# Two steps of the routing three slots later, in blocks 2 to 6

## The chip, the cores and the metric

One core of one Trainium2 chip runs the kernel. The metric is device microseconds of one execution. Engines are named as in the profile: PE (TensorE's products), PEld (its weight loads), DVE (VectorE), ACT (ScalarE), POOL (GpSimd) and SP (SyncE, which issues most DMAs).

## What is computed

Three layers in a row, over 3072 tokens of width 384:

```python
# 1: a recurrent attention, per batch (4) and head (8), 768 steps, head size 48
cur = u * k_t (outer) v_t
y_t = r_t @ (state + cur)
state = w_t[:, None] * state + k_t (outer) v_t
# 2: a gated layer, d_ff 1536
xn = x / sqrt(mean(x * x) + 1e-6) * rms_g
x = (silu(xn @ w_gate) * (xn @ w_val)) @ w_out
# 3: eight experts, each token goes to one
logits = x @ w_gate;  e_idx = argmax(logits)
gate_w = softmax(logits)[e_idx];  eom = sigmoid(x @ w_output_gate)
out[mask_e] = gate_w * eom_e * (relu(x @ w1[e]) @ w2[e])
```

## The kernel before

The tokens are cut into 24 tiles of 128, and these into eight blocks of three tiles (`for j in range(NB)`). Block j runs the gated layer on its own three tiles and, in between, the attention of the three tiles of block j + 1. The gated layer walks over 12 chunks f of d_ff: `l1` multiplies x with w_gate and then with w_val (two halves of nine products each, all at L181), and from f = 2 on `l2` multiplies the result of chunk f - 2 with w_out (nine products, also L181) into three accumulators of width 400. Each product that needs full precision is done as three with a high and a low part.

The order on every engine is written by hand. `l1` and `l2` call `slot()` at fixed points: after each half of a chunk and, from f = 2 on, after `l2`. Slots are counted from 0 in each block: 0 and 1 belong to f = 0, 2 and 3 to f = 1, 4, 5 and 6 to f = 2 (6 is behind the first `l2`), 7, 8 and 9 to f = 3, and so on. A `Plan` holds a list of generators for each slot and advances each by one step there. Whatever a step issues stands in the engines' queues at that point.

Two kinds of generators are planned in blocks 1 to 6. `attention` has nine steps per tile; its offsets are `OFFS` = 0, 1.6, 3.2, 4.8, 6.4, 8, 9.6, 11.6, 13.8, cut to whole slots, and the second and third tile start at slots 9 and 18. In short, for a tile from block 1 on: step 0 a scan on DVE (L382) and two products r, k and u on POOL (L390, L391); step 1 L394 and L395 on DVE; step 2 the second scan (L403, L406), a sum (L413), and on POOL the bonus y (L425); step 3 four transposes (L435) and L453; step 4 the scores (L461, PE) and their masks (L465, DVE); step 5, which is slot 8 for the first tile, the products that make y: with the state (L489), of the masked scores with v (L496) and of the keys with v (L478), then L504 on DVE, L508 and L510 on ACT and L513 on POOL; step 6 L520; step 7 L528 on ACT; step 8 three transposes (L532), L536 on ACT and L539 on DVE.

`route` sorts the tokens of the block before into the experts' areas. Its first step is one product with `acc` (L632, PE) and nine small operations on DVE (L639 to L657), which find each token's expert. Its second step is four products (L660, L663) that count the tokens ahead of each, seven small operations on DVE (L668 to L677), and three scatters, each a memset (L256) and an indirect DMA (L257) on POOL, which put the rows of 394 numbers, 128 at a time, into the scratch tensor `scr`. The two steps stand four slots apart. The call in block j gives the first step's slot: 24 in block 1 and 2 in all later ones. Block 7 has no attention left.

PSUM tiles of the name m come from three banks in turn, so each user waits for the reader of the third one before it.

After the eight blocks the experts run, one after another, on rows fetched from `scr`; the change does not touch them.

Of the kernel before, what the change touches and what calls it, by code (L numbers as in the profile page):

```python
# [22 lines left out]
def kernel(  # L23
# [14 lines left out]
    WINDOWS=((448,), (424,), (408,), (396,), (384,), (368,), (352,)),  # L38
    ROUTE_AT=(0, 3),
    ROUTE_STEP=3,  # L40
    WHOLE=6,
    KV_AT=0,
    KT_DVE=(0, 2, 3, 4, 5),
# [61 lines left out]
    def bank(tag, bufs, shape):  # L105
        return ps.tile(shape, F32, tag=tag, bufs=bufs, name=tag)

    def words(src):
        return src.bitcast(U32) if src.dtype != U32 else src
# [440 lines left out]
    def route_columns(k, tf):  # L550
# [11 lines left out]
        for i in range(2):  # L562
            for kk in range(KD):
                for t in (slice(0, 64), slice(64, P)):
# [3 lines left out]
                    )  # L568
        if k < WHOLE:
            nc.scalar.activation(out=whole_w[k][:, :, DM:WIDTH], in_=o, func=AF.Copy)  # L570
# [55 lines left out]
    def route(c, t0, nt, xr, last):  # L626

        b_ps = bank("m", 3, [P, E])
        nc.tensor.matmul(b_ps, c["one_b"], c["acc"], start=True, stop=True)  # L632
        base = late.tile([P, E], F32, tag="base", name="base")
        if last:
            nc.vector.tensor_tensor(out=base, in0=b_ps, in1=c["floor"], op=ALU.max)
            nc.vector.tensor_tensor(out=c["skip"], in0=base, in1=b_ps, op=ALU.subtract)
            nc.vector.tensor_tensor(out=base, in0=base, in1=c["area"], op=ALU.add)
        else:
            nc.vector.tensor_tensor(out=base, in0=b_ps, in1=c["area"], op=ALU.add)  # L639
        lo = xr[:, :, LC:LC + E]  # L640
        mx = late.tile([P, nt, 1], F32, tag="r_mx", name="mx")
        q = late.tile([P, nt, E], F32, tag="r_q", name="q")
        oh = late.tile([P, nt, E], BF16, tag="r_oh", name="oh")
        nc.vector.tensor_reduce(mx, lo, axis=AX.X, op=ALU.max)
        nc.vector.tensor_tensor(
            out=q, in0=lo, in1=mx.to_broadcast([P, nt, E]), op=ALU.is_equal
        )
        nc.vector.tensor_tensor(
            out=q, in0=q, in1=c["rev"].unsqueeze(1).to_broadcast([P, nt, E]), op=ALU.mult
        )  # L650
        nc.vector.tensor_reduce(mx, q, axis=AX.X, op=ALU.max)
        nc.vector.tensor_tensor(
            out=oh, in0=q, in1=mx.to_broadcast([P, nt, E]), op=ALU.is_equal
        )
        nc.vector.tensor_tensor(out=q, in0=xr[:, :, LC + E:WIDTH], in1=oh, op=ALU.mult)
        nc.vector.tensor_reduce(xr[:, :, ZC:ZC + 1], q, axis=AX.X, op=ALU.add)
        nc.vector.tensor_copy(xr[:, :, IC], c["ids"][:, t0:t0 + nt])  # L657
        yield
        rk = bank("m", 3, [P, nt, E])
        nc.tensor.matmul(rk, c["tri"], oh, start=True, stop=False, skip_group_check=True)  # L660
        for j in range(nt):
            for i in range(j):
                nc.tensor.matmul(  # L663
                    rk[:, j], c["one_b"], oh[:, i], start=False, stop=False, skip_group_check=True
                )
        t = late.tile([P, nt, E], F32, tag="r_t", name="t")
        si = late.tile([P, nt, 1], U32, tag="si", bufs=2, name="si")
        nc.vector.tensor_tensor(  # L668
            out=t, in0=rk, in1=base.unsqueeze(1).to_broadcast([P, nt, E]), op=ALU.add
        )  # L670
        nc.vector.tensor_tensor(out=t, in0=t, in1=oh, op=ALU.mult)
        nc.vector.tensor_reduce(mx, t, axis=AX.X, op=ALU.add)
        nc.vector.tensor_copy(si, mx)
        for j in range(nt):
            scatter(scr, E * AREA - 1, xr[:, j, 0:ROW], si[:, j])
        for j in range(nt):
            nc.vector.tensor_tensor(out=c["acc"], in0=c["acc"], in1=oh[:, j], op=ALU.add)  # L677
        yield
# [14 lines left out]
    sizes = [3] * (NT // 3)  # L693
    starts = [sum(sizes[:j]) for j in range(len(sizes))]
    NB = len(sizes)
# [31 lines left out]
    with tc.manual_schedule():  # L727

        turned = ring_view([4, KD * P], big=False)
        c = {}  # L730
# [31 lines left out]
        for f in range(KF):  # L762
# [8 lines left out]
            if f % 2:  # L771
                def whole(k=f // 2):
                    if k == WHOLE - 1:
                        whole_w[k] = p1.tile([P, 2, WIDTH], F32, name="wlast")
# [9 lines left out]
                def more(tf, k=f // 2):  # L784
# [4 lines left out]
                     words(w_out)[(f - 1) * P:(f + 1) * P, :].rearrange("(a p) n -> p a n", p=P))  # L789
                ], parted, whole if f // 2 < WHOLE else None, more))  # L790
        gens_w = []
# [4 lines left out]
        def routed_step():  # L796

            n = done_w[0]
            for k in sorted(routed):
                if k not in plan_r:  # L800
                    plan_r[k] = {n, n + 1, n + ROUTE_STEP}
                if n in plan_r[k]:
# [23 lines left out]
        def decode_step():  # L826
# [5 lines left out]
            elif len(wo) < KF // 2:  # L832
                split_wo(min(k for k in range(WHOLE) if k not in wo))
            done_w[0] += 1
# [75 lines left out]
        for j in range(NB):  # L910
            nt = sizes[j]
            n = nt * P
            plan = Plan()
            if j:
                plan.add(
                    route(c, starts[j - 1], sizes[j - 1], xr, False), 2 if j > 1 else 24,
                    (0, 4),
                )
            if j + 1 < NB:
                nxs = new_x(j + 1)  # L920
                for a in range(sizes[j + 1]):
                    plan.add(
                        attention(c, starts[j + 1] + a, nxs[0], nxs[1], a * P),
                        a * TGAP if j else 0, OFFS if j else OFF0[a],
                    )

            def slot():
                plan.step()

                if plan.slot % DSLOT[1] in DSLOT[:1] if j == 0 else plan.slot % 2:  # L930
                    decode_step()

            acc = [bank(f"l{a}", 1, [P, WIDTH]) for a in range(nt)]
            hs = {}
            for f in range(KF + 2):
                if f < KF:
                    if j == 0:
                        weights_to(f + f // 2 + 1)
                    hs[f] = l1(f, xs[0], xs[1], n, slot, j == 0 and f // 2 < WHOLE)
                if f >= 2:  # L940
                    if (f - 2) // 2 in routed:
                        exhaust(routed.pop((f - 2) // 2))
                    if j == 0 and (f - 2) // 2 < WHOLE:
                        l2_whole(f - 2, hs.pop(f - 2), acc)
                    else:
                        if (f - 2) // 2 not in wo:
                            split_wo((f - 2) // 2)
                        l2(f - 2, hs.pop(f - 2), acc)
                    slot()
                if j == NB - 1:  # L950
                    if f == 3:
                        lead = pick(c)
                        xw = expert_weights(0, lead)
                    if f >= 4:
                        next(xw, None)
                    if f == KF - 3:
                        xg0 = ring_view([EARLY // P, ROW])
                        nc.sync.dma_start(
                            out=xg0,
                            in_=scr.rearrange("(e a) c -> e a c", e=E)[ds(lead, 1), 0:EARLY, :]  # L960
                            .rearrange("o (t p) c -> p (o t) c", p=P),
                        )
                    if f == KF:
                        x0 = ring_view([2, KD, EARLY], FR)
                        transpose_in(c, xg0, EARLY, x0[:, 0], x0[:, 1])
                if j == 1 and ini < E:
                    init_rows(c, ini)
                    ini += 1
            plan.finish()
            if j == 0:  # L970
                decs.close()
                late = ctx.enter_context(
                    tc.tile_pool(name="late", bufs=1, side="right", reuse_waits="tile")
                )
                route_constants(c, late)
                pr = ph1.enter_context(tc.tile_pool(name="pr", bufs=1, reuse_waits="tile"))
            if j == NB - 2:
                rawp = ph1.enter_context(tc.tile_pool(name="rawp", bufs=3, reuse_waits="tile"))
            if j + 1 < NB:
                xr = pr.tile([P, nt, WIDTH], F32, tag="xr", name="xr")  # L980
            else:
                xr = ring_view([nt, WIDTH])
            for a in range(nt):
                if j == NB - 1 and a == 1:
                    nc.vector.tensor_copy(xr[:, a], acc[a])
                else:
                    nc.scalar.activation(out=xr[:, a], in_=acc[a], func=AF.Copy)
            if j + 1 < NB:
                xs = nxs
# [399 lines left out]
```

## Time and profile before

| | us |
|---|---|
| median of 3 runs | 864.63 |
| the runs | 863.51 to 864.8 |
| the profiled execution | 865.86 |
| its span, from the first to the last instruction | 864.2 |

| engine | busy us | share of the span |
|---|---|---|
| PE | 832.8 | 96% |
| PEld | 783.8 | 91% |
| DVE | 510.8 | 59% |
| ACT | 323.5 | 37% |
| POOL | 192.4 | 22% |

The busy time is the union of an engine's instructions; the rest of the span it was idle. Blocks 2 to 6 lie between about 204.7 and 560 us of the span, some 71 us each, and TensorE's granted clock was 1.00 of its full 2.4 GHz there. A row of the timeline gives start, duration, engine, line, operation, result<-operands, and how many instructions are merged in it; in brackets stands how long the engine had been idle and what ended that. "issue" there means that the profile shows nothing that it waited for.

### The profile page before, as it was taken

The numbers are of one execution on the slowest core, as the hardware profiler recorded it, in microseconds if no ns is written. First come the engines' busy times: TensorE is split into PE (matmuls) and PEld (weight loads), VectorE is DVE, ScalarE is ACT, GpSimd is POOL, SyncE is SP. The second block draws the span as 40 slices with busy tenths as digits, with TensorE's granted clock in tenths as the row PEclk, the third lists the DMA queues.
The fourth block names the chain that finished last, engine by engine and source line by source line (L and its number), as shares of the span: only waits on it lengthen the run. The fifth ranks groups of instructions, "written<-read, shape, count | busy, mean of one in ns | idle before, by whom it ended". The sixth has DMA issues, their size and how long they took to land. (4 is left out here: it accounts for less than half of the span.)

```text
span 864.2 us, 18816 instructions
## 1 busy us (share of the span) xinstructions
PE 832.8 (96%) x7657; PEld 783.8 (91%) x7657; DVE 510.8 (59%) x1056; ACT 323.5 (37%) x711; POOL 192.4 (22%) x248
## 2 busy tenths in 40 slices
PE   7699999999999999999999999999999999999994
PEld 5488788999999999899999989999999999999994
DVE  7798956665663764564556465243655566565651
ACT  5756543223223232233323322323434434453430
POOL 4445402222311321131032131010112022112111
PEclk9889999999999999999999999999999999999998
DMA  8954514741320221222132030022165354445510
GB/s 214 273 155 139 165 39 133 204 139 54 105 56 11 85 69 43 76 65 57 40 90 64 2 89 16 1 83 74 61 204 166 116 161 149 148 141 169 161 40 23
DMA packets 63740, 88.17 MB, mean 102 GB/s; under 512 B 5538, under 2 KB 55220, under 8 KB 63652
## 3 DMA queue, kind: packets, MB, share of 16 engines
q1 hardware_dynamic: 60014, 77.36, 31.0%
q0 software_dynamic: 3312, 9.56, 2.9%
q8 instruction: 61, 1.00, 0.5%
q14 instruction: 27, 0.22, 0.1%
q10 hardware_dynamic: 326, 0.03, 0.0%
HBM read 70.71 MB, written 16.58 MB: 101 GB/s over the span
## 5 line engine op out<-in xcount | busy, mean ns | idle before, releaser
L181 PE MATMUL a<-xh,gv 128*128 128x384 f32 x1152 | 320.7, 344 | 1.4 <-ACT xh L536 1.4
L181 PEld LDWEIGHTS a<-xh,gv 128*128 128x128 f32 x1152 | 211.8, 189 | 4.6 <-ACT xh L536 1.8
L181 PE MATMUL a<-xl,gv 128*128 128x384 f32 x576 | 194.7, 338 | 0.2 <-DVE xl L539 0.2
L181 PE MATMUL l<-wo,hh 128*128 128x400 f32 x504 | 134.2, 347 | 0.0
L602 DVE TENSOR_TENSOR sil<-a,sil 128x384 f32<-128x384 f32 x84 | 46.6, 555 | 119.0 <-PE a L181 119.0
L181 PEld LDWEIGHTS a<-xl,gv 128*128 128x128 f32 x576 | 109.1, 189 | 1.0 <-DVE xl L539 0.6
L181 PE MATMUL a<-xh,w1s 128*128 128x272 f32 (+7 forms) x384 | 106.1, 337 | 0.4 <-DVE hl L1053 0.4
L595 ACT ACTIVATE sil<-a 128x384 f32<-128x384 f32 x96 | 47.1, 491 | 158.1 <-PE a L181 155.5
L604 ACT ACTIVATE hh<-sil 128x384 fp32r<-128x384 f32 x84 | 44.1, 524 | 144.5 <-DVE sil L602 142.8
L181 PEld LDWEIGHTS l<-wo,hh 128*128 128x128 f32 x504 | 91.1, 188 | 1.3
L181 PE MATMUL l<-wo,hl 128*128 128x400 f32 x252 | 86.3, 343 | 0.0
L1053 DVE SCALAR_TENSOR_TENSOR hl<-a,hh 128x256 fp32r<-128x256 f32 (+8 forms) x72 | 38.6, 539 | 68.3 <-ACT hh L1052 64.5
L257 POOL DMA_INDIRECT out_dram<-row,iu x30 | 35.4, 1179 | 189.4 <-DVE row L1064 146.4
L181 PEld LDWEIGHTS a<-xh,w1s 128*128 128x128 f32 x384 | 69.9, 188 | 2.0 <-DVE hl L1053 0.7
L1052 ACT ACTIVATE hh<-a 128x256 fp32r<-128x256 f32 (+8 forms) x72 | 34.5, 479 | 94.2 <-PE a L181 92.6
L181 PE MATMUL l<-hh,rows 128*128 128x272 f32 (+4 forms) x240 | 67.5, 346 | 0.0
L607 DVE TENSOR_TENSOR hl<-sil,hh 128x384 fp32r<-128x384 f32 x84 | 46.7, 556 | 31.9 <-ACT hh L604 31.9
L181 PE MATMUL a<-xl,w1s 128*128 128x272 f32 (+7 forms) x192 | 64.6, 336 | 0.1
L425 POOL TENSOR_TENSOR y<-vt,g 128x384 f32<-128x384 f32 x19 | 17.3, 911 | 161.7 <-issue 61.5
L513 POOL TENSOR_TENSOR ss<-ss,mhalf 128x1 f32<-128x1 f32 x24 | 14.3, 597 | 153.7 <-ACT ss L510 151.7
L181 PEld LDWEIGHTS l<-wo,hl 128*128 128x128 f32 x252 | 47.2, 187 | 0.0
L181 PE MATMUL l<-rows,hh 128*128 128x384 f32 (+2 forms) x176 | 45.5, 340 | 0.0
(250 smaller groups left out, 1328.5 us busy)
## 6 DMA issues: line engine op xcount, KB each, us to landing
raw<-in_moe_w_dram SPq DMA_DIRECT2D x64, 384.0 KB
set<-in_feat_dram SPq DMA_DIRECT2D x46, 192.0 KB
rk<-in_rkv_dram SPq DMA_DIRECT2D x18, 384.0 KB
scr<-zrow SPq DMA_DIRECT2D x8, 788.0 KB
set<-in_feat_dram SPq DMA_DIRECT2D x46, 96.0 KB
vt<-in_rkv_dram SPq DMA_DIRECT2D x23, 192.0 KB
raw<-in_moe_w_gate_dram SPq DMA_DIRECT2D x8, 384.0 KB
raw<-in_moe_w_val_dram SPq DMA_DIRECT2D x8, 384.0 KB
```

Of the source, the lines that this page charges most:

```text
L181: nc.tensor.matmul(o, a, b, start=start and i == 0, stop=stop and i == 2, skip_group_check=True)
L257: ins = nc.gpsimd.indirect_dma_start(out=dst, out_offset=bass.IndirectOffsetOnAxis(ap=idx, axis=0), in_=rows, in_offset=None, bounds_check ...
L425: nc.gpsimd.tensor_tensor(out=y, in0=vv, in1=g.unsqueeze(2).to_broadcast([P, H, D]), op=ALU.mult)
L513: nc.gpsimd.tensor_tensor(out=ss, in0=ss, in1=c["mhalf"], op=ALU.pow)
L595: nc.scalar.activation(out=sil, in_=o, func=AF.Silu)
L602: nc.vector.tensor_tensor(out=sil, in0=pg[1], in1=sil, op=ALU.mult)
L604: nc.scalar.activation(out=hh, in_=sil, func=AF.Copy)
L607: nc.vector.tensor_tensor(out=hl, in0=sil, in1=hh.bitcast(F32), op=ALU.subtract)
L1052: nc.scalar.activation(out=hh, in_=o, func=AF.Relu)
L1053: nc.vector.scalar_tensor_tensor(out=hl, in0=o, scalar=0.0, in1=hh.bitcast(F32), op0=ALU.max, op1=ALU.subtract)
```

## The change

The first slot of `route` is read from a new table: 24 in block 1 and 2 in block 7, as before, and 5 instead of 2 in blocks 2 to 6. The second step follows four slots later as before, so in these blocks it moves from slot 6 to slot 9. The new table is a line of its own, so that all later lines of the kernel after have numbers higher by one.

```diff
     ROUTE_STEP=3,
+    ROUTED=(24, 5, 2),
     WHOLE=6,
@@
             if j:
                 plan.add(
-                    route(c, starts[j - 1], sizes[j - 1], xr, False), 2 if j > 1 else 24,
-                    (0, 4),
+                    route(c, starts[j - 1], sizes[j - 1], xr, False),
+                    ROUTED[0 if j == 1 else 2 if j == NB - 1 else 1], (0, 4),
                 )
```

On DVE, block 2, from slot 6 to slot 9 before. L668 to L677 are the route's second step, L465 the first tile's masks, L504 its sum into y, L520 its state, L382 the second tile's scan, L602 and L607 belong to `l1`:

```order
L668 TENSOR_TENSOR t<-m,base 128x24
L671 TENSOR_TENSOR t<-t,oh 128x24
L672 TENSOR_REDUCE mx<-t 128x3
L673 CAST si<-mx 128x3
L677 TENSOR_TENSOR acc<-acc,oh 128x8 x3
L465 TENSOR_TENSOR am<-m,tri 128x512 x2
L602 TENSOR_TENSOR sil<-a,sil 128x384
L504 TENSOR_TENSOR y<-m,y 128x4x48 x2
L607 TENSOR_TENSOR hl<-sil,hh 128x384
L520 TENSOR_TENSOR states<-m,states 48x4x48 x2
L382 SCALAR_TENSOR_TENSOR kq<-set_81,back 128x516
```

The same place after, with line numbers higher by one:

```order
L466 TENSOR_TENSOR am<-m,tri 128x512 x2
L603 TENSOR_TENSOR sil<-a,sil 128x384
L505 TENSOR_TENSOR y<-m,y 128x4x48 x2
L608 TENSOR_TENSOR hl<-sil,hh 128x384
L669 TENSOR_TENSOR t<-m,base 128x24
L672 TENSOR_TENSOR t<-t,oh 128x24
L673 TENSOR_REDUCE mx<-t 128x3
L674 CAST si<-mx 128x3
L678 TENSOR_TENSOR acc<-acc,oh 128x8 x3
L521 TENSOR_TENSOR states<-m,states 48x4x48 x2
L383 SCALAR_TENSOR_TENSOR kq<-set_81,back 128x516
```

The second step's seven operations have moved from ahead of the masks to behind the sum into y, and they now stand ahead of the state and the scan.

On POOL, block 2, before. The three pairs of a memset and a DMA are the scatters, L425 is the first tile's bonus and L513 its root mean square, L390 belongs to the second tile:

```order
L425 TENSOR_TENSOR y_2680<-vt_2199,g_2676 128x384
L256 MEMSET pad_2739 1x1
L257 DMA scr_66<-xr_2587,si_2734 25600x394
L256 MEMSET pad_2744 1x1
L257 DMA scr_66<-xr_2587,si_2734 25600x394
L256 MEMSET pad_2749 1x1
L257 DMA scr_66<-xr_2587,si_2734 25600x394
L513 TENSOR_TENSOR ss_2865<-ss_2865,mhalf_129 128x1
L390 TENSOR_TENSOR rk_2678<-rk_2678 128x384
```

And after:

```order
L426 TENSOR_TENSOR y_2665<-vt_2199,g_2661 128x384
L514 TENSOR_TENSOR ss_2836<-ss_2836,mhalf_129 128x1
L257 MEMSET pad_2862 1x1
L258 DMA scr_66<-xr_2587,si_2857 25600x394
L257 MEMSET pad_2867 1x1
L258 DMA scr_66<-xr_2587,si_2857 25600x394
L257 MEMSET pad_2872 1x1
L258 DMA scr_66<-xr_2587,si_2857 25600x394
L391 TENSOR_TENSOR rk_2663<-rk_2663 128x384
```

The scatters have moved from ahead of the first tile's root mean square to behind it; they still stand ahead of the second tile's first product.

## Rows read from the trace of the kernel before

**Rows 1.** The page's first part: busy time, share of the span, instructions.

```profile
PE 832.8 (96%) x7657; PEld 783.8 (91%) x7657; DVE 510.8 (59%) x1056; ACT 323.5 (37%) x711; POOL 192.4 (22%) x248
```

**Rows 2.** PE's waits in blocks 2 to 6: total us, times, longest us.

```profile
PE m L496 <- issue: 5.1, 12, 0.5
```

**Rows 3.** Timeline around the first tile's products, block 2, then block 6.

```profile
220.67 0.68 PE L489 MATMUL m<-states,rq 48*64 48x48 f32 x32
221.27 0.97 POOL L257 DMA_INDIRECT scr<-xr,si  x1 [0.22 <-issue]
221.28 0.49 PE L496 MATMUL m<-vt,am 128*32 128x48 f32 x13
222.24 0.30 PE L496 MATMUL m<-vt,am 128*32 128x48 f32 x5 [0.47 <-issue]
222.96 0.70 PE L496 MATMUL m<-vt,am 128*32 128x48 f32 x44 [0.42 <-issue]
...
223.97 0.62 PE L181 MATMUL l<-wo,hh 128*128 128x400 f32 x2
...
505.22 0.97 POOL L257 DMA_INDIRECT scr<-xr,si  x1 [0.25 <-issue]
...
506.88 0.72 PE L496 MATMUL m<-vt,am 128*32 128x48 f32 x44 [0.44 <-issue]
```

**Rows 4.** Windows' sums, blocks 2 to 6: first tiles' products, then second tiles'.

```profile
sum 16.97, PE 11.91; mean PE 2.38
...
sum 8.50, PE 8.50; mean PE 1.70
```

**Rows 5.** DMA queues during block 2's scatters; a block 1 window (length, busy, clock, DMA).

```profile
q0 software_dynamic: 192, 0.61, 30.3%
...
168.41:170.97 2.56, 2.02 (x129) 1.00 1.02 233
187.54:189.31 1.77, 1.77 (x129) 1.00 0.06 20
```

**Rows 6.** Timeline of block 1: a scatter beside transposes.

```profile
196.83 0.97 POOL L257 DMA_INDIRECT scr<-xr,si  x1 [0.23 <-issue]
...
197.63 0.49 PE L532 MATMUL m<-ident,y 128*128 128x128 f32 x3
```

**Rows 7.** Timeline of PE in block 7, the route's second step.

```profile
568.47 0.34 PE L181 MATMUL l<-wo,hl 128*128 128x400 f32 x1
568.65 0.19 PE L660 MATMUL m<-oh,tri 128*128 128x24 bf16 x1
...
568.77 0.42 PE L181 MATMUL a<-xh,gv 128*128 128x384 f32 x1
```

**Rows 8.** Timeline of blocks 1 and 2: the route's operations and the chain behind slot 9.

```profile
192.92 0.18 DVE L668 TENSOR_TENSOR t<-m,base 128x24 f32<-128x24 f32 x1 [2.10 <-PE m L663]
...
193.65 0.59 DVE L677 TENSOR_TENSOR acc<-acc,oh 128x8 bf16<-128x8 bf16 x3
...
208.42 0.66 DVE L395 TENSOR_TENSOR kq<-set,kq 128x512 f32<-128x512 f32 x1
...
224.73 0.72 DVE L520 TENSOR_TENSOR states<-m,states 48x192 f32<-48x192 f32 x2
226.84 1.23 DVE L395 TENSOR_TENSOR kq<-set,kq 128x512 f32<-128x512 f32 x1
227.60 1.34 POOL L391 TENSOR_TENSOR rk<-rk,u_bc 128x384 f32<-128x384 f32 x1
229.11 0.56 DVE L602 TENSOR_TENSOR sil<-a,sil 128x384 f32<-128x384 f32 x1 [1.04 <-PE a L181]
230.13 0.60 ACT L528 ACTIVATE y<-y,ss 128x384 f32<-128x384 f32 x1
232.04 0.49 PE L532 MATMUL m<-ident,y 128*128 128x128 f32 x3
232.61 0.55 DVE L413 TENSOR_REDUCE g<-rk 128x8 f32<-128x384 f32 x1
```

## The prediction

> **What bounds the kernel now.** I read the page's first part, then TensorE's waits, then the timeline around the places where the route steps stand. TensorE (PE) is busy 832.8 of 864.2 us [rows 1], so a change matters only if it makes PE wait less or more. In blocks 2 to 6, the stretch from 204.7 to 560 us, PE waits in one place only: L496, the products of the masked scores with v, 5.1 us in 12 gaps, the longest 0.5 us, with no engine named as releaser [rows 2].
>
> The timeline shows that place [rows 3]. In block 2 the first tile's products begin at 220.67 with L489 (32 rows; the trace has two rows for each of these products), go on at 221.28 with 13 rows of L496, and then stop: 0.47 us of nothing, five rows, 0.42 us of nothing, and at 222.96 the rest in one go. The block's next product with the weights (L181) starts only at 223.97. On GpSimd (POOL) the scatters of the route's second step run at the same time, the third and last of them from 221.27 to 222.24. The last gap ends 0.72 us after the third scatter's row; in block 6 it is 506.88 against 505.22 + 0.97 = 506.19, so 0.69 us. The other three blocks lie between. The second tile of the same block and the third, without a scatter near them, have no gap.
>
> The price is more than the idle time, since the five rows between two gaps count as busy. One group gives it whole [rows 4]. The five first tiles' stretches, from the first L489 to the next L181, last 16.97 us together; the same stretches of the second tiles, in the same blocks with the same products, 8.50 us, all of it busy. The difference is **8.47 us**, some 1.7 us in each block.
>
> What PE lacks in the gaps the trace does not say. DMA traffic as such is a weak suspect: between 218.69 and 223.97 the DMA engines carried only the scatters, 192 packets at 30.3% [rows 5]; in block 1 a stretch beside loads and zero rows at a share of 1.02 lasted 2.56 us, 0.79 longer than the 1.77 of the next one, without that traffic. So other traffic can cost something too, but the scatters cost twice as much at a third of the traffic.
>
> **The change part by part.** No instruction is added or taken away; both route steps move, each three slots later, in five blocks. Block 1 and block 7 keep their slots.
>
> *The second step's scatters, slot 6 to slot 9.* On POOL they now stand behind L513 of the first tile. They wait for DVE's L677, which waits for the route's own products, which PE reaches only after the first tile's products and nine more products with w_out. So they cannot run beside this stretch any more. Gain: 8.47 if the stretch falls to the second tiles' length. What could be left of the excess: nothing by the second tiles [rows 4], up to 0.79 per block by the stretch in block 1 [rows 5], which is 3.95 in all. I take nothing left, as the traffic before 223.97 was the scatters' alone.
>
> *Where the scatters go instead.* From slot 9 on PE runs L181 products. Under the scatters it still got five rows in 0.72 us (222.24 to 222.96), 0.144 us each; an L181 product takes 0.18 us (568.47 to 568.65) [rows 7], so it asks for less than it was given. In block 1 a scatter at 196.83 stands over three transposes L532 at 197.63 and PE does not idle [rows 6]. In the new place the last scatter may meet the seven small products of slot 13 (L532, L435). At 0.144 each they take 1.01 us, of which L532's row of 0.49 us [rows 8] is spent anyway: at most 0.5 per block, 2.6 in all. I take 0, because PE got through 45 rows in [rows 3] before it stopped, and here are seven.
>
> *The route's own products on PE.* In block 7 the second step's four take 0.30 us from one L181 to the next (568.47 plus 0.18 to 568.77 leaves 0.12 for them) [rows 7]. They leave one place and enter another of the same kind: net 0, with 0.12 either way as the bound, for two steps and five blocks 1.2 us either way.
>
> *The first step's nine operations on VectorE (DVE), slot 2 to slot 5.* They now stand behind L602 of the third chunk and ahead of L465, where before the second step's seven stood ahead of L465. One step replaces the other in front of the masks that PE needs at L496; I take 0.
>
> *The second step's seven operations on DVE, slot 6 to slot 9.* They take from 192.92 to 193.65 + 0.59 = 194.24, 1.32 us [rows 8]. They now stand ahead of L520 and of the second tile's scan L382. I count in block 2's old time, so that PE stays put. PE ends the nine products at 223.97 + 9 x 0.18 = 225.6 and the route's at 225.9. DVE ends the seven at 227.2, where before it started L520 at 224.73: 2.5 us later. From L520 to the end of L395 it took until 226.84 + 1.23 = 228.07, and then it idled 1.04 us before L602 at 229.11. So L602 is 1.5 us late, and L528 on ScalarE with it: it ends at 230.13 + 0.60 + 1.5 = 232.2, and PE wants it at 232.04 for L532. That would be 0.2 us lost per block, 1.0 in all. But L395 took only 0.66 where POOL was idle (208.42), and POOL's products L390 and L391, which ran beside it, now come later; with 0.66 L528 ends at 231.7 and nobody waits. I take 0 and keep 1.0.
>
> *POOL's queue.* Behind the scatters stand L390 and L391 of the second tile, which DVE's L413 reads. L391 ended at 227.60 + 1.34 = 228.94, L413 began at 232.61 [rows 8]. Three scatters of 0.97 us with a memset ahead of each, some 3.7 us begun about 227.5, let L390 begin at 231.2 and L391, which L390 delays by as much as before, end near 234.2 (an estimate from these rows), so L413 waits perhaps 1 us. What is late behind it is DVE's next L602. It frees a bank that PE writes again only after 18 more products, the nine with w_out and the nine of the next first half, 18 x 0.18 = 3.2 us later. I take 0. SP's and ScalarE's orders do not change.
>
> The sum: 8.47 saved, 0 given back. The profiled execution took 865.86 us (span 864.2 and 1.66 around it), so the changed kernel would take 857.39 by its clock. The median of the three runs is 864.63, 1.23 below that; the forecast is 864.63 - 8.47 = **856.2 us**, about 1.0% faster.
>
> **A rule that speaks against it.** The stretch and the scatters share the time, and there is 1.7 us of delay wherever they do [rows 3, 4]. The Trainium skill's page "SBUF — State Buffer", section "SBUF: two separate sides", says that engine ports and DMA ports are disjoint, so that a DMA and a compute operation cannot slow each other. By the rows the sum is 856.2; by that rule alone the scatters' data would cost PE nothing and moving them would leave 864.6. The trace does not contradict the rule on ports, as its gaps name no operand, but it does contradict the conclusion.
>
> **The rivals.**
>
> *The gaps stay where they are.* The stall would belong to the first tile itself, to the place in the program, not to the scatters. For it: the gap comes after 12 or 13 rows of L496 in all five blocks. Against it: its end follows POOL by 0.69 to 0.72 us in each. Then nothing is gained: 864.6 us, which is also where the rule just named would leave it.
>
> *Part of it stays or moves.* Loads meet the stretch (3.95), the seven small products of slot 13 starve (2.6), or L532 waits (1.0). Each alone leaves a gain of 4.5 to 7.5, so 857.2 to 860.1 us; the first with the 1.2 of the route's products leaves 861.3.
>
> *The DVE chain turns the sign.* The second step stands ahead of L520, L382 and L395, and its 2.5 us reach PE at L532 in full if the 1.04 us of idle time ahead of L602 and the spare behind it vanish. It decides from 1.7 us per block, where it eats the gain. In full: 5 x (2.5 - 1.7) = 4 us slower, 868.6 us. Against it: 1.0 of the 2.5 is idle time that the row itself shows, and L528 has another 1.3 us before L532.
>
> **How the numbers follow.** The forecast 0.75, part of it 0.13, the gaps stay 0.07, the DVE chain 0.05. Runs of one kernel differ by about 0.2%, 1.7 us, which is the least that a measurement can tell from no change. Faster by more than that: the first two, 0.88; the same 0.07; slower 0.05. The range: below, 8.47 and 1.2 from the route's products, 855.0 us; above, the forecast with what loads could leave (3.95) and the wait at L532 (1.0), 861.1 us, which takes in nearly all of the second case and leaves out the last two.
>
> **What would show it.** Right: in the changed profile the first tiles' stretches in blocks 2 to 6 last 1.8 us (1.4 in block 6) without a gap, TensorE's waits lose the L496 line of 5.1 us, and the scatters run beside L181. The DVE chain shows as a wait of PE at L532 for ScalarE's L528, starved transposes as gaps at L435 or L532. Wrong: gaps in L496 that stand where they stood while POOL has no scatter near, or PE's saved time found again as waits in slots 10 to 15.

## The result

The changed kernel takes 856.69 us (median of 6 runs, 855.61 to 857.51), the kernel before 864.52 on the same chip (863.51 to 864.8): 7.83 us less, a ratio of 0.9913 with a 95% interval of 0.99 to 0.9926. The forecast was 856.2. This gain was measured in that group of runs alone; in another, as the experiments show, the two kernels are 0.6 us apart.

The changed kernel has one line more at its head, so its lines, and those quoted of it, are one higher than before's; the experiments have before's numbers, or those with their own lines added.

The first part of the page, as in [rows 1], of the kernel after:

```profile
span 854.9 us, 18804 instructions
...
PE 829.9 (97%) x7657; PEld 781.3 (91%) x7657; DVE 516.6 (60%) x1056; ACT 323.5 (38%) x711; POOL 191.4 (22%) x248
```

The span is 9.3 us shorter, more than the medians say. Of this, 1.1 us lie ahead of the change: the last tile's products of block 1 end at 189.31 before [rows 5] and at 188.18 here. PE's waits from 203 to 560 us have no line left; the 5.1 us of [rows 2] are gone. The windows of the five first tiles' products, as in the first sum of [rows 4], of which the first is shown (length, PE busy, rows in brackets, granted clock, DMA share, GB/s):

```profile
219.39:221.16 1.77, 1.77 (x129) 1.00 0.00 0
...
sum 8.51, PE 8.51; mean PE 1.70
```

16.97 us have become 8.51, the length of the second tiles before, and no DMA moves in them. The timeline of block 2, PE and then POOL, answers [rows 3]:

```profile
219.39 0.68 PE L490 MATMUL m<-states,rq 48*64 48x48 f32 x32
220.01 0.89 PE L497 MATMUL m<-vt,am 128*32 128x48 f32 x64
220.71 0.52 PE L479 MATMUL m<-vt,kt 128*32 128x48 f32 x32
221.16 0.63 PE L182 MATMUL l<-wo,hh 128*128 128x400 f32 x2
...
224.30 1.06 POOL L258 DMA_INDIRECT scr<-xr,si  x1 [1.09 <-DVE acc L678]
225.67 1.50 POOL L258 DMA_INDIRECT scr<-xr,si  x1 [0.22 <-issue]
227.48 0.97 POOL L258 DMA_INDIRECT scr<-xr,si  x1 [0.23 <-issue]
```

All 64 rows of L497 run in one go, and the scatters begin 3.1 us after the stretch has ended, beside L182, which shows no gap. From one product's start to the next, none of the L182 products between the first and the second tile of blocks 2 to 6 takes over 0.01 us longer than before, but for the one behind the route's own products.

### The profile page after: what moved, and what is told of

It is laid out like the page before. It is cut to its first block, busy times and chain, and to the rows that moved or that the text cites. A ratio compares the mean times of both kernels' runs of the same rounds, so it can differ in the third digit from the quotient of the medians.

```text
span 854.9 us, 18804 instructions
## 1 busy us (share of the span) xinstructions
PE 829.9 (97%) x7657; PEld 781.3 (91%) x7657; DVE 516.6 (60%) x1056; ACT 323.5 (38%) x711; POOL 191.4 (22%) x248
## 5 line engine op out<-in xcount | busy, mean ns | idle before, releaser
L182 PE MATMUL a<-xh,gv 128*128 128x384 f32 x1152 | 320.9, 344 | 1.4 <-ACT xh L537 1.4
L182 PEld LDWEIGHTS a<-xh,gv 128*128 128x128 f32 x1152 | 211.9, 189 | 4.6 <-ACT xh L537 1.8
L182 PE MATMUL a<-xl,gv 128*128 128x384 f32 x576 | 194.9, 338 | 0.2 <-DVE xl L540 0.2
L182 PE MATMUL l<-wo,hh 128*128 128x400 f32 x504 | 134.6, 348 | 0.0
L182 PEld LDWEIGHTS a<-xl,gv 128*128 128x128 f32 x576 | 109.2, 189 | 1.1 <-DVE xl L540 0.6
L182 PE MATMUL a<-xh,w1s 128*128 128x272 f32 (+7 forms) x384 | 106.2, 337 | 0.4 <-DVE hl L1054 0.4
L182 PEld LDWEIGHTS l<-wo,hh 128*128 128x128 f32 x504 | 90.8, 188 | 1.3
L182 PE MATMUL l<-wo,hl 128*128 128x400 f32 x252 | 86.3, 343 | 0.0
L182 PEld LDWEIGHTS a<-xh,w1s 128*128 128x128 f32 x384 | 69.8, 188 | 2.0 <-DVE hl L1054 0.7
L608 DVE TENSOR_TENSOR hl<-sil,hh 128x384 fp32r<-128x384 f32 x84 | 51.7, 615 | 28.9 <-ACT hh L605 28.4
L182 PE MATMUL l<-hh,rows 128*128 128x272 f32 (+4 forms) x240 | 67.5, 346 | 0.0
L182 PE MATMUL a<-xl,w1s 128*128 128x272 f32 (+7 forms) x192 | 64.5, 336 | 0.1
L182 PEld LDWEIGHTS l<-wo,hl 128*128 128x128 f32 x252 | 47.2, 187 | 0.0
L182 PE MATMUL l<-rows,hh 128*128 128x384 f32 (+2 forms) x176 | 45.5, 339 | 0.0
```

Source lines behind the costliest of these rows:

```text
L182: nc.tensor.matmul(o, a, b, start=start and i == 0, stop=stop and i == 2, skip_group_check=True)
L608: nc.vector.tensor_tensor(out=hl, in0=sil, in1=hh.bitcast(F32), op=ALU.subtract)
```

## The experiments

The edits are against the kernel before; in all but the two repeats, block 1 and block 7 keep their slots. Each group ran on one chip, and the five groups on five chips; which chip gave the result and the first trace is not on record. No chip is known to have been used twice, so the chip cannot be told from whatever else may differ between groups, such as where the program was put in memory. "A chip" below stands for a group of runs.

### Which of the two steps

The edits here are of the two numbers with which `plan.add` takes the route's plan in blocks 2 to 6: the slot of the first step, and the way from it to the second.

**The second step alone.**

```diff
-2, (0, 4)
+2, (0, 7)
```

> Blocks 2 to 6: the first step stays at slot 2, the second goes to slot 9. Theory (the scatters beside the first tile's products are the whole gain): all first tiles' stretches from L489 to the next L181 last 1.77 us (1.43 in block 6), time 856.2 to 856.7, no slower than the changed kernel; the first step in its old place saves at most the 0.1 us a block that its product L632 costs more ahead of l2. Rival (the first step's nine operations of DVE ahead of the masks, or its product, matter too): stretches stay at 2.5 us or more and the time lies above 859.

Measured: 856.95 us (856.64 to 857.62), all first tiles at 1.77 us (1.43 in block 6). That looks like the theory. But the kernel before took 857.03 on this chip (856.11 to 859.54), not 864.5, so the time tells nothing: there was hardly anything to gain.

**The first step alone.**

```diff
-2, (0, 4)
+5, (0, 1)
```

> Blocks 2 to 6: the first step goes to slot 5, the second stays at slot 6. Theory: the scatters still run beside the first tile's products, so the stretches last 3.3 to 3.6 us and the time is that of the kernel before, 864.5, within 0.2%; DVE has both steps ahead of the masks, which could cost 0.5 us a block more, up to 867. Rival (moving the first step is what frees PE): stretches of 1.77 us and 856.7.

Measured: 862.13 us, 5.1 us slower than the kernel before on that chip (ratio 1.0057, 1.0044 to 1.0071). Both expectations missed. The stretches were 1.43 to 2.03 us. The loss has another cause, in PE's waits (total us, times, longest us):

```profile
PE m L660 <- DVE oh L652: 4.3, 5, 1.2
```

With one slot between the steps, PE comes to the second step's products before DVE has made what they read, the first step's L652. One slot between the steps is too few; numbers between one and four were not run.

**The second step ahead of the second tile's products.**

```diff
-2, (0, 4)
+5, (0, 10)
```

> Blocks 2 to 6: the first step at slot 5 as in the changed kernel, the second at slot 15, two slots ahead of the second tile's products as it was two slots ahead of the first tile's before. Theory: the first tiles' stretches stay at 1.77 us, the second tiles' rise from 1.77 to 3.3 to 3.6 us with gaps in L496, and the time is back at 864.5. Rival (the gap belongs to the first tile's place in the program): second tiles stay at 1.77 us, 856.7.

Measured: 856.68 us, ratio 0.9992 (0.9984 to 1.0001), second tiles at 1.77 us. The 864.5 of the theory did not come, here as in the first run. The placing was also weak: POOL's last scatter in block 2 ends as L496 begins.

```profile
238.34 0.98 POOL L257 DMA_INDIRECT scr<-xr,si  x1 [0.23 <-issue]
...
239.43 0.89 PE L496 MATMUL m<-vt,am 128*32 128x48 f32 x64
```

**A fiftieth of the bytes, first try.** In the kernel before, with `scr8` a tensor of its own:

```diff
-            scatter(scr, E * AREA - 1, xr[:, j, 0:ROW], si[:, j])
+            if 0 < t0 < starts[NB - 2]:
+                scatter(scr8, E * AREA - 1, xr[:, j, 0:8], si[:, j], False)
+            else:
+                scatter(scr, E * AREA - 1, xr[:, j, 0:ROW], si[:, j])
```

> The kernel before, but in blocks 2 to 6 each scatter moves 8 numbers per row instead of 394, into a scratch tensor of its own, so these tokens' rows never reach the experts. As many indirect DMAs with as many row indices, 2% of the bytes. If the bytes in flight starve PE: stretches of 1.8 to 2.0 us and 856 to 857. If making the descriptors on POOL starves it: stretches of 3.3 us or more as before, 864.5.

Measured: 857.06 us in one run, first tiles at 2.07 to 2.09 us. It does not decide, since the three scatters also waited for each other; it is repeated below.

### The same two kernels on another chip

> The kernel before, unchanged, once more with a trace, since on the chip of the first four experiments it took 857.0 us and not 864.5. Theory now: the scatters' place is needed for the gap but is not enough, and whether PE's supply of instructions suffers under them depends on the chip or on where the program lies. On a chip where the kernel before takes 864.5 the first tiles' stretches last 3.3 to 3.6 us; where it takes 857.0 they last 1.8 to 2.1 us with the scatters at the same place beside them. Rival: the 857.0 come from somewhere else in the program and the stretches are at 3.3 us there too.

> The changed kernel, unchanged. Its time does not depend on the chip, 856.7 within 0.2%, as no scatter runs beside small products: stretches of 1.77 us (1.43 in block 6). Where the kernel before takes 857.0, the two are the same within 0.2%. Rival: it is faster there too by about 0.9%, near 849, if the whole chip is faster.

> The second step two slots ahead of the second tile's products, once more. On a chip where the kernel before takes 864.5: second tiles' stretches of 3.3 to 3.6 us and 864.5 in all. On one where it takes 857.0: 1.77 to 2.1 us and 856.7, as in the first run. Rival (the gap belongs to the first tile): 1.77 us on either.

Measured, on the next chip: the kernel before 857.29 us, the changed one 856.65, beside 857.27 for another copy of the kernel before; the ratio of the changed one is 0.999 (0.9981 to 1.0). The second step at slot 15 took 856.57, again with second tiles at 1.77 us. So the changed kernel takes the same time here as on the first chip, and it is the kernel before that differs. Its five first tiles here:

```profile
219.72:221.69 1.97, 1.97 (x130) 1.00 0.33 126
...
sum 9.62, PE 9.61; mean PE 1.92
```

9.62 us instead of 16.97, with the scatters at the same place beside the products: 1.1 us over the 8.51 without them. This fits the second theory: the place of the scatters is needed for the loss, but how much they cost differs from one chip, or group of runs, to another. Two copies of the kernel before agree within this group (857.29 and 857.27 us).

### Scatters nearer, and none

The second step one slot later than in the kernel before:

```diff
-2, (0, 4)
+2, (0, 5)
```

> Blocks 2 to 6: the first step at slot 2, the second at slot 7, one slot later than before, so that the three scatters begin about when the first tile's products do. Theory (POOL's scatters starve the small products; how much depends on the chip): on a chip with 857 for the kernel before, stretches of 1.9 to 2.5 us and up to 3 us more than the changed kernel's 856.7; on a chip with 864.5, stretches of 3.3 us or more and 864 or more. Rival (on this kind of chip the scatters cost nothing and the 0.2 us a block came from elsewhere): 1.77 us and 856.7.

And the kernel before without the scatters of these blocks:

```diff
-            scatter(scr, E * AREA - 1, xr[:, j, 0:ROW], si[:, j])
+            if not 0 < t0 < starts[NB - 2]:
+                scatter(scr, E * AREA - 1, xr[:, j, 0:ROW], si[:, j])
```

> The kernel before with its slots, but without the 15 scatters of blocks 2 to 6, so the tokens of five blocks never reach the experts. Theory: nothing runs beside the first tiles' products, so stretches of 1.77 us (1.43 in block 6), and the time is that of the changed kernel less 0.5 us, near 856.1, on any chip. Rival (the gap belongs to the place, not to the scatters): the stretches stay as long as the kernel before's on the same chip.

Measured, beside 857.29 for the kernel before: at slot 7, 857.79 us, ratio 1.0008 (0.9998 to 1.0017); without the scatters, 854.76, ratio 0.9967. The sums of the first tiles' windows, slot 7 and then without:

```profile
sum 9.29, PE 9.28; mean PE 1.86
```

```profile
sum 8.51, PE 8.51; mean PE 1.70
```

Without scatters the excess is gone in all five blocks, so it is theirs on this kind of chip too. At slot 7 the sum has hardly changed (9.29 against 9.62), but the blocks have. Block 2, then block 6:

```profile
219.28:221.47 2.19, 2.18 (x129) 1.00 0.25 92
497.71:499.14 1.43, 1.43 (x98) 1.00 0.00 0
```

In block 2 two of POOL's scatter rows lie nearly whole in the stretch, and its 2.19 us are the longest first tile of blocks 2 to 6 on this kind of chip. In block 6 it is the first row alone, from 497.71 to 498.77, no data move yet, and there is no excess at all. So one scatter's row beside the products is not enough. The kernel without scatters is 2.5 us faster, 1.3 more than expected; some 1.5 us of it lies at the very end, behind PE's last product, and was not followed up.

### The second tile, on a chip of the first kind

```diff
-2, (0, 4)
+5, (0, 11)
```

> Blocks 2 to 6: the first step at slot 5, the second at slot 16, one slot ahead of the second tile's products, so that the scatters run beside these and not beside the first tile's. Theory on a chip with 864.5 for the kernel before: first tiles at 1.77 us, second tiles at 3.3 us or more with gaps in L496, 863 to 866 in all. On a chip with 857: second tiles at 1.8 to 2.2 us, first tiles at 1.77, 856.5 to 858. Rival (the excess belongs to the first tile): second tiles at 1.77 us on either kind of chip.

Measured: 876.66 us (874.95 to 877.67), beside 864.84 for the kernel before on the same chip: 1.0136 (1.0118 to 1.0155). This chip behaves as the first one did. The windows' sums, first tiles and then second tiles:

```profile
sum 8.49, PE 8.49; mean PE 1.70
```

```profile
sum 23.71, PE 14.78; mean PE 2.96
```

The loss has left the first tiles and gone to the second tiles, with the scatters: 23.71 us against 8.50, 15.2 us more. That refutes the rival by which the gap belongs to the first tile. The first step stands at slot 5 here as in the changed kernel, so the loss goes with the second step; neither step was moved alone on this kind of chip. The loss is also larger than at the first tiles, where part of the scatters ran ahead of the stretch; here nearly all of their time lies in it. Block 2, PE and POOL:

```profile
237.38 1.06 POOL L257 DMA_INDIRECT scr<-xr,si  x1 [6.14 <-DVE acc L677]
...
239.43 0.31 PE L496 MATMUL m<-vt,am 128*32 128x48 f32 x6 [0.44 <-issue]
...
240.01 0.97 POOL L257 DMA_INDIRECT scr<-xr,si  x1 [0.22 <-issue]
...
241.68 0.55 PE L496 MATMUL m<-vt,am 128*32 128x48 f32 x30 [0.43 <-issue]
```

PE crawls, four to six rows in some 0.75 us, until 0.70 us after the last scatter's row (240.98 to 241.68), as in [rows 3]. In all ten stretches with gaps, these five and before's five, PE first gets 44 to 48 rows and only then three to six at a time, whether POOL's first scatter begins 0.5 us ahead of the stretch, as here, or 1.5 to 2.0 us ahead, as in the kernel before. That looks like a stock that runs out with a slow supply behind it; no run tests this reading.

The trace is that of the execution of 874.95 us. From block 2's first tile to block 6's third tile it takes 331.63 us, against 312.74 in the changed kernel: 18.9 more, of which the stretches explain 15.2. The rest, 3.7, is the clock, which has a small part in the 15.2 too. The windows of the nine products with w_out behind the second tile, blocks 2, 3 and 4 (length, PE busy, rows, clock, DMA share, GB/s):

```profile
242.71:245.79 3.08, 3.08 (x12) 0.52 0.26 69
316.61:318.35 1.74, 1.74 (x15) 1.00 0.31 68
389.33:392.48 3.15, 3.15 (x12) 0.50 0.27 68
```

After the bursts and gaps the granted clock fell to the lower of PE's two levels, 1.2 GHz instead of 2.4, in blocks 2, 4 and 6, and the nine products take 3.08, 3.15 and 2.65 us instead of 1.74: 1.3, 1.4 and 0.9 us lost. In blocks 3 and 5 it did not fall, after bursts and gaps of the same kind.

### Bytes, or the making of the DMAs

Small rows as above, but without waits among the three, since the helper's list of earlier scatters has one entry for each tensor's kind of rows:

```diff
-            before = scattered.setdefault(bound, [])
+            before = scattered.setdefault((bound, first), [])
...
+                scatter(scr8, E * AREA - 1, xr[:, j, 0:8], si[:, j], "small")
```

In the other kernel there is no indirect DMA in blocks 2 to 6, but nine plain ones that SP issues:

```diff
+        if 0 < t0 < starts[NB - 2]:
+            nc.vector.tensor_tensor(out=xr[:, :, IC], in0=c["ids"][:, t0:t0 + nt], in1=mx[:, :, 0], op=ALU.max)
+            for j in range(3 * nt):
+                nc.sync.dma_start(out=scr9[j * P:(j + 1) * P, :], in_=xr[:, j % nt, 0:ROW])
```

> The kernel before with its slots; in blocks 2 to 6 each scatter moves 8 numbers per row instead of 394, into a tensor of its own, and the three no longer wait for one another, as they did in the first run of this kind. The tokens of five blocks never reach the experts. If the bytes in flight are what PE suffers from: stretches of 1.8 us at most 1.9 on any chip. If it is POOL's making of the indirect DMAs: stretches as long as the kernel before's on the same chip, 3.3 us where that takes 864.5 and 1.9 to 2.1 where it takes 857.

> The kernel before with its slots; in blocks 2 to 6 the scatters are replaced by nine plain DMAs of the same rows, three times the bytes, issued by SP behind DVE's L677, so that POOL makes no DMA there and no row is routed. If the bytes are what PE suffers from: stretches of 3.3 us or more where the kernel before takes 864.5, 2.0 or more where it takes 857. If it is POOL's making of the indirect DMAs: 1.77 us, at most 0.2 more.

Measured, beside 857.75 for the kernel before: small rows 857.06 us, nine plain DMAs 854.52. The windows of the first tiles, small rows and then plain DMAs; the last two columns are DMA share and GB/s:

```profile
219.22:221.15 1.93, 1.93 (x130) 1.00 0.02 2
...
sum 9.49, PE 9.47; mean PE 1.90
```

```profile
219.33:221.10 1.77, 1.77 (x130) 1.00 1.04 365
...
sum 8.70, PE 8.70; mean PE 1.74
```

With a share of 0.02 the excess is nearly all there (9.49 against 9.62); with full DMA engines but nothing made by POOL it is nearly gone (8.70 against 8.51, and all but 0.01 of that in block 5). On this kind of chip, then, what PE suffers from goes with POOL's indirect DMAs and not with their bytes or with the load on the DMA engines. Which part of them it is, their making on POOL, their queue or their 128 separate rows, is open: the two kernels differ in all three, and in the run at slot 7 a scatter's row on POOL alone cost nothing in block 6.

On the other kind neither kernel was run. The trace of the kernel before has a hint for its bytes, in block 2 behind POOL's last row, which ends at 222.24 [rows 3]:

```profile
222.24:222.70 0.46, 0.30 (x5) 1.00 0.00 0
222.96:223.47 0.51, 0.51 (x44) 1.00 0.68 257
```

First PE gets five rows while no data move, and then 44 in one go while the third scatter's data do. In the other four blocks, too, the rows behind the last gap run beside a DMA share of 0.73 or 0.74. So data on their way to memory do not hold PE back there either.

## Why the prediction was right

**The scatters leave the stretch: 8.47 us.** Right on the chip it was read from: 16.97 became 8.51. What the prediction took for a property of the kernel is one of kernel and chip, or group of runs, together. Of the six groups of runs two had 864.5 to 864.8 for the kernel before, four had 857.0 to 857.8. Where it was traced on the latter, the same term is 1.1 us, and a gain of 8.47 forecast there would have been nearly 8 us off (857.29 to 856.65 instead of 848.8). One trace could not show that, so it was luck that the result was taken on the chip of the trace. The gaps without a releaser could have been a hint that something outside the program sets their size. What differs between the chips is not known. It is not the granted clock, 1.00 in the first tiles' stretches of both kinds. The 61 instruction packets of 16 KB in the traces come at nearly the same places of the program, and PE's waits in blocks 2 to 6 differ in the one line of L496.

**Where the scatters go.** Right: taken at 0, and there is no gap at L182, L533 or L436.

**The route's own products: taken at 0, bound 1.2.** Mis-sized: it is a loss of 0.5 us. From the end of block 1's last stretch to that of block 6's last it takes 542.65 - 189.31 = 353.34 us before and 533.56 - 188.18 = 345.38 after, 7.96 less, so 0.5 of the 8.46 is given back. With it the sum comes out: 864.52 - 8.46 + 0.50 = 856.56, and 856.69 were measured. The step that failed is that the second step enters a place of the same kind as the one it left. Block 2, before and then after:

```profile
215.88 0.35 PE L181 MATMUL l<-wo,hl 128*128 128x400 f32 x1
216.07 0.19 PE L660 MATMUL m<-oh,tri 128*128 128x24 bf16 x1
```

```profile
214.71 0.34 PE L182 MATMUL l<-wo,hl 128*128 128x400 f32 x1
214.98 1.16 PE L462 MATMUL m<-rq,kq 48*128 48x128 f32 x16
...
222.72 0.34 PE L182 MATMUL l<-wo,hl 128*128 128x400 f32 x1
222.90 0.19 PE L661 MATMUL m<-oh,tri 128*128 128x24 bf16 x1
...
223.02 0.42 PE L182 MATMUL a<-xh,gv 128*128 128x384 f32 x1
223.28 0.33 PE L182 MATMUL a<-xl,gv 128*128 128x384 f32 x1
```

The old place is a switch from long products to the scores. Without the step between them, the last long product takes 0.27 us to the start of the scores, where it took 0.19 to the start of L660, so leaving this place gives back less than the step cost there. The new place costs 0.30 - 0.18 = 0.12 us, as in [rows 7], and 0.08 more in the product behind it, which takes 0.26 us to the next start instead of 0.18. Over the five blocks the way to the first tile, in which the first step moves and the second is gone, became 0.12 to 0.17 us shorter, and the way from the first tile to the second, with the second step in it, 0.18 to 0.24 longer; some 0.08 more lie behind the second tile in two of them.

**The DVE chain.** Right in its mechanism: late, and not late enough. The prediction had L528 end 0.34 us before PE wants it. Measured, in block 2's timeline of DVE, ACT and PE after:

```profile
223.92 0.57 DVE L678 TENSOR_TENSOR acc<-acc,oh 128x8 bf16<-128x8 bf16 x3
226.53 0.68 DVE L396 TENSOR_TENSOR kq<-set,kq 128x512 f32<-128x512 f32 x1
228.26 0.60 ACT L529 ACTIVATE y<-y,ss 128x384 f32<-128x384 f32 x1
...
229.45 0.49 PE L533 MATMUL m<-ident,y 128*128 128x128 f32 x3
...
232.53 0.54 DVE L414 TENSOR_REDUCE g<-rk 128x8 f32<-128x384 f32 x1
```

L529 ends at 228.86, and PE's L533 starts at 229.45 without a wait: 0.59 us to spare. L396 took 0.68 as taken, not 1.23.

**POOL's queue.** No harm, but not by the steps given. L413 (now L414) was to wait 1 us for POOL; it did not. In block 2 L392 ended at 230.79, and DVE came to L414 only at 232.53, since two of its own operations had become longer, as the last part shows.

**The rivals.** The gap's belonging to the first tile fell with the run at slot 16. A part that stays or moves did not come: the five stretches carry no DMA and no excess, and the seven small products show no wait. The DVE chain did not turn the sign either. One reading was a little off: the last gap ends 0.67 us behind POOL's row in block 3 (294.03 against 293.36), outside the 0.69 to 0.72 given for all five.

## What to carry to other kernels

Where an engine that is always busy runs many tiny instructions, look at what POOL does beside them: here indirect DMAs from POOL held back PE's small products, and the long products beside them lost nothing. Put such DMAs beside long products. Where they stand matters: on chips of the first kind, slot 9 instead of 6 saved 7.8 us, and slot 16 lost 12. And before a gap without a named releaser is taken for the kernel's own, time the kernel on a second chip.

## What the runs showed of the hardware that was not expected

The cost of the same 15 scatters beside the same products is 1.1 us on one kind of chip (9.62 against 8.51) and 8.5 us on the other (16.97 against 8.51); nothing in the traces says why.

Two DVE operations have become longer in the changed kernel, which puts 5.8 us more on DVE's busy time. Block 2, usual lengths and then those beside POOL's products of the second tile:

```profile
210.31 1.22 DVE L404 TENSOR_TENSOR_SCAN rq<-set,front 128x516 f32<-128x516 f32 x1
...
221.48 0.55 DVE L608 TENSOR_TENSOR hl<-sil,hh 128x384 fp32r<-128x384 f32 x1
...
228.38 1.55 DVE L608 TENSOR_TENSOR hl<-sil,hh 128x384 fp32r<-128x384 f32 x1 [0.59 <-ACT hh L605]
229.85 2.03 DVE L404 TENSOR_TENSOR_SCAN rq<-set,front 128x516 f32<-128x516 f32 x1
```

And POOL, in the same stretch:

```profile
228.46 1.04 POOL L391 TENSOR_TENSOR rk<-rk 128x384 f32<-128x384 f32 x1
229.58 1.21 POOL L392 TENSOR_TENSOR rk<-rk,u_bc 128x384 f32<-128x384 f32 x1
```

Before, the second of POOL's two (L391 then, L392 now) took 1.34 us, the first took 1.59 instead of 1.04, and the DVE operation that doubled was L395 (now L396), from 0.66 to 1.23 [rows 8]. The Trainium skill's page "SBUF — State Buffer", section "SBUF: two separate sides", says that VectorE, in an operation with two SBUF inputs, and GpSimd, in one that reads SBUF, share a pair of ports which one holds for a whole instruction while the other waits. The trace agrees: L608 reads two tiles of SBUF and gains 1.0 us beside L391's 1.04 us, L404 gains 0.8 beside L392. Which of the two gets the ports first the rows do not settle: L608 starts 0.08 us ahead of L391 and is still the one that becomes longer. So the move has changed which operations pay, and DVE now pays more and POOL less.
